# Three instead of four plain float32 units for each of the first two chunks, with a new order table

## The chip, the core and the metric

The kernel runs on one core of a Trainium2 chip. A core has five engines with queues of their own, each worked off strictly in order: TensorE (PE, matmuls into PSUM), VectorE (DVE), ScalarE (ACT), GpSimd (POOL) and SyncE (SP), which here only issues DMAs. The metric is the device time of one execution in microseconds; lower is better.

## What is computed

A local attention with block summaries, and a feed-forward layer on its result. Cut to what matters:

```python
B, H, S, D = 4, 8, 768, 64;  block, window = 32, 16;  scale = 1 / sqrt(D)
k_sum, v_sum = max of k, mean of v over each block of 32 positions
scores_l = scale * q @ k.T                 # only where |i - j| < window
scores_s = scale * q @ k_sum.T + log(block)
a = softmax(concat([masked scores_l, scores_s]))
x = (a @ concat([v, v_sum])).reshape(3072, 512)
h = x @ w_in                               # 512 -> 2048
out = (h * sigmoid(h)) @ w_out             # 2048 -> 512
```

The weights come in as float64 bit patterns. The kernel turns them into float32 on the chip, and then into scaled pairs of fp16 numbers (a high part and the rest).

## The kernel before

**Tiling.** The 3072 tokens are 24 stages of 128 (six for each batch element) and 12 chunks of 256. A stage is the attention of its 128 tokens, in four steps of two heads (`job_a`: scores, exponential, turning; `job_c`: the product with v; `job_x`: the result as an fp16 pair, xh and xl). The hidden width of 2048 is cut into eight pieces f = 0 to 7 of 256. A **unit** is one chunk with one piece (`job_f`, 96 units): two halves of the first product (line 908, 12 fp16 matmuls each), tanh on ScalarE (922), a multiply on VectorE (923), then the second product (917) in two calls, one for each 128 tokens, which adds to the chunk's output banks.

**Two kinds of units.** A unit can run its second product in two ways. The ordinary way casts the activations to fp16 (927), subtracts to get the rest (928), and multiplies fp16 pairs: three matmuls for each half. It needs the second weight as an fp16 pair, and all of these pairs share one scale `kap`, for which the sums of all eight second weights (line 836) and the largest values of all eight first weights (842/844, brought to all rows by the small matmul 848 and read by 852) must be there: lines 865 to 878, with a matmul of its own at line 868. The plain way needs no `kap`: it scales the float32 activations by the first weight's factor (925) and multiplies float32 by float32. The constant `QF` says for how many pieces the first two chunks use the plain way. These chunks run their pieces 0 to QF-1 first (chunk 0, then chunk 1), close the sum and put it aside (938), run the rest later (chunk 1, then chunk 0) and add the two sums (949). Chunks 2 to 11 run all pieces in one go, in fp16.

```python
    first = list(range(NFP))[:QF]
    rest = list(range(NFP))[QF:]
    runs = [(c, first) for c in range(NSUP)] + [(c, rest) for c in reversed(range(NSUP))]
    runs += [(c, first + rest) for c in range(NSUP, NCHUNK)]
    ...
        plain = c < NPW and f < QF
    ...
            terms = ((g, plain_w[f, 1]),) if plain else ((gh, wt[f, 1][:, 0]), (gh, wt[f, 1][:, 1]), (gl, wt[f, 1][:, 0]))
```

**Preparing a weight** (`job_w`): one DMA of 1 MB (816), three bit operations that make float32 of the two halves (826 on ScalarE, 822 on GpSimd, 820 on ScalarE or 824 on VectorE, 828 on VectorE), the sum or maximum, and the split into fp16 (`split_w`: 860 on ScalarE, 861 on VectorE; the profile shows them by the helpers' lines, 266 and 273). Unit f of the first product needs its first weight split; a plain unit needs its second weight as float32 only.

**The order.** The kernel first lists all its operations with their dependencies and with the engines that may run each (`plan.op`). The table `ORDER` then gives the sequence and the engine: three base-36 digits for each operation, five times its number plus the engine. `replay` walks the table, works out planned times from fixed costs, and puts filler matmuls (line 389) where TensorE would idle at the start. Each engine's queue has its operations in the order of the table. SP's queue holds all 276 DMAs. The dictionary `TUNE` feeds priorities that count only when no table of the right length is there.

**Shared places.** The small matmuls of the early part (848, 868, and those of the scales) write one PSUM bank, so each waits until the reader of the one before (852 for 848) is done. Weight pieces that are loaded late lend their memory to the first four stages for keys and values.

Of the kernel before, what the change touches and what calls it, by code (L numbers as in the profile page):

```python
# [251 lines left out]
def local_attn_ffn(ctx: ExitStack, tc: tile.TileContext, q0, qkT, qF, qD, kF, kD, v, vR, w, out):  # L252
# [782 lines left out]
    "12i0k30jt0k50iz0td12p0tj0km0jb0jj0kr0kw0uc0uf0l10kc0l40lu12v0fw0lc0g210l10q1nh0um11t1250ux10v0lz0md0no0ne0nu0mu0n00gp0kf"
    "0g81cw1nm0mk1nu0mq0n212y0nk0nw0v51md0v10n91mk0lg1201d10vi0o40vc1d91290vu0w11dd0o60on0w70od0p71dj1dv1e00oj1dl0ph0pd0pn0ot"
    "0pp0wa0wg0ur1e80vl0ov0q60wk0wn0qb0qg0pw0p30wu0x50xd0xq0x10y21n41dq0y91ec0lm0m91uz0pz0ql0qo1mt12f0yd0x91eu0qw0yi1101ei0ls"
    "1uw1ez0xk1f70yn14q14x0ys0yv0r00r61330z21ne1up1411ek1ep1fb1fh1nz1v71ud1690zd1530xt0z70vr16g0ra13a11311a1560zh14814e1vy1w4"
    "14h1fo0zl0zx1h216y1h71hf0zs1751hj1hp1o215b16m1ft1fy1fj1g61mn13b15g1um1ga17b1hw13i15j1j010118h18s18o1wa17e1gg1gn0xz16p107"
    "17k17q14n1wd1la1lm16v1wj1i11i61ie15q18x1931ii1io1hr1v91ve1vm16111l1m417r17y1971gi19c19f1vp19m19r19w1a11a61j51jd1vw1x71xd"  # L1040
    "1xj1o51om1oc1891oi1jh1mx1iv1jz1jn1q01n71pq1r215x1ab1q61ag1cp1ar1os16518d1ju11p1ws1wp1k41iq1wy1r911h2bs1ow2bn1p11p61pd1kc"
    "1kg2bi1ct1pg2bd1rj1zt1zy1pk1pw1qa13t13x1av1km1kt20x21213n1c51bv1bz1sx1x41lr1cf2061l61rp1jp1mb1ko20a20g20m1xm20s22122621a"
    "21e1y61yd1sn1st21k1qf1qp1xw1y31c92cc21o1qk1cj21w1qu1xt1yh1rf1rt1ym1ry1s31u51t31l122e1t718322i22o1qy1sa1bb2cr1yp1sd1sh1yw"
    "1tc1ti1tn1z11z61zb1h023523a23i1zg1zl1bl1zq2bz20n21r22s1bf23m23023s2cj22v1tr1tv1al2c323w2cn2dq2cy2441bp23z2d224b24l1tz2p3"
    "1b124w2501uf1lh2e12dw2p82pg2pk25325a25k2pq26o2pw25g2e524f26y2eg2q72eb2qc25q25u24p2d82qk2qo1gv25z26b2qu2r028028h28728d2db"
    "2dm2dh2ek2652q226e2rb2ng26u27427828n28r29l27d27k29v26i2rg2ro27o2gn2rs2px2r62sf2r127s2a129r2ry2sk2a52aa2al28w2eq2s427w2f3"
    "2ag2ap2at29729229b2ev29f2sa2fa2f02fd2ss2sw2t22fk2s52nn2c82fp2fu2hb2fz2g42ax2nv2hi2t82ho2b52hs2g92t91b52iu2b92hy2i22gs2gz"
    "2h42i72nr2jb2jh2j12j72ie2ij2im3ac2ha2iq3ah2kd3ap2ku2kk2te3bg2lw2l03at2tl2tv3bl3az3b53bb2of2ok2kq2l42l92o22o62lf2tp3bt3bx"
    "2jl2jq2tz2oc2k23ck2m33cp2md2u33c33c73cf3do2jv3cx2k530x3d12ua2uk3d72gg2uq2vm2os2ll3db2lo2ls2m92ug2uu2mj2mn3dt2ow2p031c3e1"
    "3e53143183b63eb2ms38p2vt2n43dj2w32my2n72nb3es2k92uz3ex3f52x52xc3f931w2xm2vz3213eh3ca3de2v92v52ve3en2vi3ff3fj2w92yo31j31n"  # L1050
# [120 lines left out]
```

## Time and profile before

| what | us |
|---|---|
| median of three runs | 612.56 (612.44 to 612.84) |
| the profiled execution | 612.63 |
| its span, first to last instruction | 610.9 |
| TensorE busy | 605.8 |
| VectorE busy | 466.9 |
| ScalarE busy | 391.5 |
| GpSimd busy | 139.7 |

The span is what the trace shows; 1.73 us of the execution's time lie around it. A busy time is the time in which at least one instruction of the engine ran, so the overlapping of pipelined matmuls is not counted twice, and the mean of a matmul's record is longer than the distance to the next. Pieces of the chain of waits show that distance. A line number is that of the kernel's text, for copies and scalings that of the helper (258 to 276).

### The profile page before, as it was taken

Reading aid. Unit: us, or ns where it says so; the run is one execution under the profiler, and the core shown is the slowest. Engines: PE = TensorE matmul, PEld = TensorE weight load, DVE = VectorE, ACT = ScalarE, POOL = GpSimd, SP = SyncE. Lnnn points to the kernel's source line nnn. Section 1 sums busy time; section 2 is a strip of 40 time slices with the busy share of each in tenths; the row PEclk is TensorE's granted clock in tenths of the full one; section 3 lists DMA queues with packets and bytes.
Section 4 is the critical chain, followed back from the end, with each engine's and each line's share of the span. In section 5 each row is a group of like instructions: output and inputs, shape, how many; then the busy total and the mean of one; then the engine's idle time right before and its main releaser. Section 6 shows DMA issues by size and latency. Waiting matters only on the chain.

```text
span 610.9 us, 13765 instructions
## 1 busy us (share of the span) xinstructions
PE 605.8 (99%) x5085; PEld 427.6 (70%) x5085; DVE 466.9 (76%) x1384; ACT 391.5 (64%) x866; POOL 139.7 (23%) x172
## 2 busy tenths in 40 slices
PE   8999999999999999999999999999999999999997
PEld 5786756677676776767777676767767667666785
DVE  7998978999889766897888846997788876753321
ACT  3999989667776667655787567644665655442222
POOL 2333321023314301413303341112422012101000
PEclk9999999999999999999999999999999999999999
DMA  8999615764666754583775764685565652502100
GB/s 310 342 335 382 248 40 167 172 158 114 191 137 141 202 172 142 158 210 82 195 145 130 173 194 136 152 197 124 98 161 130 143 131 64 87 14 57 53 2 35
DMA packets 91560, 93.50 MB, mean 153 GB/s; under 512 B 70348, under 2 KB 72652, under 8 KB 89444
## 3 DMA queue, kind: packets, MB, share of 16 engines
q1 hardware_dynamic: 91492, 92.62, 56.0%
q8 instruction: 40, 0.66, 0.5%
q14 instruction: 28, 0.23, 0.1%
HBM read 68.12 MB, written 6.29 MB: 122 GB/s over the span
## 4 chain that ended last, share of the span: by engine, by line
PE 94%; DMA 3%; ACT 1%; SPq 0%; DVE 0%; issue 0%
PE bank L917 42%; PE bank L908 41%; PE bank L762 4%; PE bank L676 2%; PE bank L677 2%; DMA wt<-in_w_dram 1%; DMA wt<-in_kF_dram 1%; PE bank L746 1%; DMA wt<-vms 1%; PE bank L674 1%; PE bank L671 0%; ACT wt L826 0%; ACT e L691 0%; PE bank L389 0%; PE bank L460 0%
## 5 line engine op out<-in xcount | busy, mean ns | idle before, releaser
L917 PE MATMUL bank<-wt,g 128*128 128x512 f16 (+2 forms) x1168 | 278.6, 382 | 0.0
L908 PE MATMUL bank<-xh,wt 128*128 128x256 f16 x1536 | 273.9, 273 | 0.0
L908 PEld LDWEIGHTS <-wt 128*128 128x128 f16 x2304 | 224.1, 98 | 45.1 <-issue 3.3
L908 PE MATMUL bank<-xl,wt 128*128 128x256 f16 x768 | 209.3, 273 | 0.0
L917 PEld LDWEIGHTS <-g 128*128 128x128 f16 x1104 | 106.7, 98 | 95.3 <-issue 0.8
L922 ACT ACTIVATE t<-bank,asc 128x512 f32<-128x512 f32 x96 | 65.7, 684 | 90.0 <-PE bank L908 89.7
L923 DVE SCALAR_TENSOR_TENSOR t<-t,bank 128x512 f32<-128x512 f32 x96 | 65.5, 683 | 55.7 <-ACT t L922 55.1
L691 ACT ACTIVATE e<-e,mx 128x182 f32<-128x182 f32 x192 | 83.8, 438 | 29.2 <-DVE mx L688 28.9
L927 ACT CAST g<-t 128x512 f16<-128x512 f32 x88 | 54.1, 615 | 49.4 <-DVE t L923 46.3
L726 DVE SCALAR_TENSOR_TENSOR p<-e,sum,p 128x128 f16<-128x128 f32 x320 | 80.1, 313 | 2.9 <-POOL p L715 1.7
L276 POOL TENSOR_TENSOR g<-t,g 128x512 f16<-128x512 f32 x31 | 35.9, 1158 | 161.3 <-ACT g L927 77.5
L688 DVE CUSTOM_DVE_ANT_0 e<-bank,masks,qsc 128x182 f32<-128x182 f32 x144 | 54.0, 402 | 21.0 <-PE bank L677 19.0
L715 POOL TENSOR_SCALAR p<-e,sum 128x182 f16<-128x182 f32 x45 | 24.6, 549 | 119.1 <-DVE sum L708 23.5
L276 DVE TENSOR_TENSOR g<-t,g 128x512 f16<-128x512 f32 x57 | 39.7, 696 | 12.0 <-ACT g L927 11.3
L691 ACT ACTIVATION_READ_ACCUMULATOR e<-e,mx 128x1 f32 x192 | 36.1, 188 | 0.0
L713 ACT ACTIVATE p<-e,sum 128x182 f16<-128x182 f32 x65 | 26.6, 437 | 14.1 <-DVE sum L708 7.4
L276 POOL TENSOR_TENSOR vv<-raw,vv 128x1024 f16<-128x1024 f32 x12 | 25.6, 2133 | 15.6 <-DVE p L717 5.9
L571 DVE SCALAR_TENSOR_TENSOR qk<-raw,qsc,qk 64x1264 f16<-64x1264 f32 x18 | 27.6, 1535 | 2.0 <-ACT qk L570 1.4
L676 PE MATMUL bank<-qk 128*128 128x182 f16 x144 | 28.7, 241 | 0.0
L677 PE MATMUL bank<-qk 128*128 128x182 f16 x144 | 28.7, 242 | 0.0
L570 ACT ACTIVATE qk<-raw,qsc 128x1264 f16<-128x1264 f32 x18 | 24.1, 1340 | 5.1 <-DMA raw<-in_kD_dram 5.1
L566 DVE SCALAR_TENSOR_TENSOR qk<-raw,qsc,qk 128x1024 f16<-128x1024 f32 x18 | 23.7, 1316 | 3.7 <-ACT qk L565 3.6
(169 smaller groups left out, 640.1 us busy)
## 6 DMA issues: line engine op xcount, KB each, us to landing
wt<-in_w_dram SPq DMA_DIRECT2D x16, 1024.0 KB
raw<-in_kD_dram SPq DMA_DIRECT2D x18, 632.0 KB
raw<-in_v_dram SPq DMA_DIRECT2D x20, 512.0 KB
raw<-in_qD_dram SPq DMA_DIRECT2D x18, 512.0 KB
out_dram<-raw SPq DMA_DIRECT2D x23, 256.0 KB
raw<-in_kF_dram SPq DMA_DIRECT2D x12, 384.0 KB
raw<-in_qF_dram SPq DMA_DIRECT2D x9, 512.0 KB
raw<-in_vR_dram SPq DMA_DIRECT2D x12, 384.0 KB
```

What stands on the lines that cost most here:

```text
L276: eng[e].tensor_tensor(out=out, in0=in0, in1=in1, op=ALU.subtract)
L571: plan.op({"dve": 1450}, lambda e: nc.vector.scalar_tensor_tensor(out=kst[64:, :, :NLOC], in0=kr[64:], scalar=qs[64:, 1:2], in1=kst[64:, : ...
L676: nc.tensor.matmul(out=sc[:, i, :NKEY], lhsT=qh[:, h, :], rhs=kst[:, h, :], start=True, stop=False)
L677: nc.tensor.matmul(out=sc[:, i, :NKEY], lhsT=ql[:, h, :], rhs=kst[:, h, :], start=False, stop=True)
L688: plan.op({"dve": 258 if b == 0 else 323}, lambda e, i=i: nc.vector.tensor_tensor_reduce(out=et[:, i, :NKEY], in0=sc[:, i, :NKEY], in1=mas ...
L691: plan.op({"act": 431}, lambda e, i=i, h=h: nc.scalar.activation(out=et[:, i, :NKEY], in_=et[:, i, :NKEY], func=AF.Exp, scale=-1.0, bias=m ...
L726: nc.vector.scalar_tensor_tensor(out=pt[:, i, to:to + z - a], in0=et[:, i, a:z], scalar=su[:, i:i + 1], in1=pt[:, i, a:z], op0=ALU.mult, o ...
L908: nc.tensor.matmul(out=h[:, d * CH:(d + 1) * CH], lhsT=wt[f, 0][:, part, d, ct * P:(ct + 1) * P], rhs=x[:, ct, :], start=(ct == 0 and q == ...
L917: nc.tensor.matmul(out=bank[to][:, :z0 - a0], lhsT=a[:, d * CH + u * P:d * CH + u * P + P], rhs=b[:, d, a0:z0], start=(opens and d == 0 an ...
L922: plan.op({"act": 640}, lambda e: nc.scalar.activation(out=t, in_=h, func=AF.Tanh, scale=asc_t[c // 3 % 2][:, f:f + 1]), r=[("bank", k), ( ...
L923: plan.op({"dve": 605}, lambda e: nc.vector.scalar_tensor_tensor(out=t, in0=t, scalar=1.0, in1=h, op0=ALU.add, op1=ALU.mult), r=[("bank", ...
L927: plan.op({"act": 540}, lambda e: nc.scalar.copy(out=gh, in_=t), r=[("t", j)], w=[("gh", n)], prio=at - TUNE["post"])
```

## The change

`QF` goes from 4 to 3. Piece 3 of chunks 0 and 1 is then an ordinary fp16 unit and is run with the late pieces: chunk 0 and chunk 1 each have three plain units and five ordinary ones. Each of the two units has two operations (927, 928) in the place of one (925), so the list has 2530 operations instead of 2528, and they are numbered anew. The early sums are closed behind piece 2 instead of piece 3.

`ORDER` is replaced as a whole. Read back by number, every operation runs on an engine that its `plan.op` allows, as before; the lists of allowed engines are not changed. Of the 2522 operations that both tables have, 204 go to another of their allowed engines. TensorE keeps 536 operations and SP 276; ScalarE goes from 642 to 653, VectorE from 926 to 912, GpSimd from 148 to 153. In SP's queue the 16 weights come in another sequence, and two key pieces of the second batch element stand among them earlier than before. The end of the table (chunk 11) differs in the order of the last calls, and two of its three last evictions move from ScalarE to VectorE.

```diff
-QF = 4
+QF = 3
...
 ORDER = (
-    "1lw00700l00r1lz00b00h01f01k00405p02401p02f01t05w02801507006q06206600v01b07601106c06e0av06w06m02j03d02u07807g07i02n07z085"
...
-    "9q09qn9qq9ow9qg9q59qx9r0"
+    "0041jc1jw00b1kd00h00l01f01k00r05p01p02001t06606q06c06w07005w06206e07601501b00v01102402f07802j02u00803d06m07i07z08t07g0av"
...
+    "9q59qm9qq9qa9qx9r09p69qf9r69ra"
 )
```

More of the change, by code (lines that the diff above doesn't have):

```diff
@@ L1035 @@
[L1035 to L1050, printed above, removed]
@@ new lines @@
+    "02807p07v0aq0b902n08j08p03s04302y0390850870bq08z0910bw03o0bg0bm0320by0ck09i09808f04d1k10d209n09s09x0re0rl05g03h03w0cq0ca"
+    "0cg0c50ed0ej0e30e90dj0dp0d90rr0df0ru0rz0el0cs0dr0dy0sx0b00ta0490et04g04n04s0t40s60f204x0f70520570fc0d005c0fh0gf0ga0gt0ha"
+    "0tm0tt0tz0hg0i40ia0s71uf0se0sl0hu0i00gk0h00h60a00sp0a705l09b0hi0ic0hq0ik0im0u20ac0ai0st11t10a0ao1200u70jx0it10h10n0j30jn"
+    "0k30fk0fr0ue0jt0j90td0b50lz0ev0k50iz0km0uf0kr0kw0jb0l11kn0kd0um0fw12i0l412612p0lu0jj0lb10q0md0mu0mk0no0g20ne12u0ux0g812y"
@@ new lines @@
+    "0gp1290kf0lg1lj1cw0nu0mq0n00n20m40v50vi0nk0nw0o30vc0na1d10o60v11dv1e010w1100ut1u00vu0p70w10ph1sf0w71d90od1lh0lm0pn1dd0pd"
+    "0m90on0pp0wa1lo0lq0ot0oj0q60ov0vl1dj1dl14q0wg1e81kz0wk0qb0p20pw1lw0qg0wn14x0wu0ql0y20y90x50qo1u60yf0x11ec1ei1kf0xd0tj0yi"
+    "0zl0yo0x90xo0xk0zs0zx1t90qv0pz0r00r61m10ys0xt1m41dq1eu14114814c1ez0ra1ep1531f70yv0z21fb0vr12f1ek1011l91fh16915616g16m1jo"
+    "11311a1g31g815b1gg18h1gk18o1fo1h218u1071331381s71h713b16p15g1fj13i18x15j1gq14h1gx1i116y17517a17e15q16v0z91tb1tg11h1to193"
@@ new lines @@
+    "1hf17j1i617q17r1gs1hj0zd0zh13p17y0xz14n19719c19f1hp1hw1kv1sn1ul1tt19m1kp1m719r1uc1xv1y019w1sz1l513t1a11a613x1ie1ur1v911l"
+    "1ab1ns1ag1ii1c51sh1ty1uu1me1io1mo1o21y81vf11p1vl1w81vo1yc1611an1mk1c91651mu1my1p41pl1yi1yo1v02at2ao1pb1iv1j81bl1bp1cf1cj"
+    "1yz1z42ay1v61wo1n31na1vy1zc1zg1o81ny1oc1hr1nd1bv1zm1iq1vv1oh1ot1on1yu2032081j21yp1bz1wf2bx1zq1zy1t11ow1w51ni1wj1wr1qz183"
+    "1k81qp1nm21720g1zt20k1wy15v21c1x31pr1x81xd1qv1ph1pv1q01r51r91xi1xn1re20q1xs1q61p02bi20u2122aj20x1qb1qf1rp1rk1rt18918d21k"
@@ new lines @@
+    "21o2bp2bt1qj22b22g21u21y2c42c81cp22o1rx1s12421b12cw1ct1fw24622122s2261jt1b524924g22y26423426a24q25u24w2602db2dm26e2o92oe"
+    "2b526j2d226v2om2oq2ow2p21sr23523h23l23a23r1ar24m27627d27n1av1g125025523v25h2d725b25k29128r2ch2ft2pd2pi2pq2pu2p827j27t27x"
+    "2822p32dh28x2cn2mm2qh2qm2q02q62qc2q726p1jj2972qu2cs2dq29b29g2rl2rq29r29m26y2qy2722b92ni2r429v1bb2dw2e92ra25o2rb2mt2e12eg"
+    "2e62ej28828d28h2rg2eq2ce2gh2sp2su2ry2s22ev2f02f529z2be2s82gy2h42go2gu2n12n82i02mx2fa2ff2h82sc2fy2hd2ih28l2a32i72jj2sk2sf"
@@ new lines @@
+    "2nc2k02jq2g52ga2ab2af2t23am2t62gg2nl2nq2ho2fk2hj2hs2l22l93ar2jw2lj2ud2tc2ti2in2k62id2to1bf2ir2iw2tj2lp2lf2j62j33bq3az3b3"
+    "3b92jb2uk2u52tv2nx2o22uu3bf3bv3c32ka3bl2kf2kk2kp2ku2o82vw2w32wd3cu3c73cd3cz3bg2xf2tz3ch3cp3ck2lt2jf3d72ly2m92u92m43db3dh"
+    "2md2xw2xm3173dn2w93dy2wj2wn31e2v031i2ws2uq2v42v92xs2y22y62yb3232hw2vk2vf2yy2vo31m3e33eb31t3dt2zf2zl2z52zb2wy2ky3ef3el3do"
+    "2x331x3f23f72zp38z32u2mh39v3ep3ex3g62x733b2zu3ff3013fj3fp33134d2yn33h3043gb3ft3g13es2yh2yq39e34k34u3963gj3gn30939l34q337"
@@ new lines @@
+    "39p35035433l35w36d3633gt3gz32632b3fw2vs33q3ha34036j37f33x34537m3593hf3hn3h53692xb35f2yu3hr30d30h36n34936s36y3h02fp37w39a"
+    "3k235k35o35s3qw3hx3i337432i32n32t39y30z37s30p3ie3kj3k93ll3a33ij31330t37737b3ls3m238238638b3ir3iv38n3i94473n438g38q3nb38u"
+    "3kf3j13j73nl3r33r73sk3kp44c3m83nh44k3i43on3j83kt3ky3la44o3l33ld44u4503ou3jd3ju3p43ly3lh45b45g3jy3jl4564513mc3jo3rv3nr3p0"
+    "3mh3ms3nv46f46k45o3aa45s45y3mm3mw3o03n03pa3pe3pj46246a3af3o63aj3rb3s03ob3of3oj46546s46w47247j47o3pq3sq3sw3pv3py3q247647e"
@@ new lines @@
+    "4793ri3rm47w3tt48048648c3s73tz3sz3u53us3t53q63tb48n48s3sd3sg3te48i4904943qo3qs49a49r49w3uz49e49m3tk4a44a83tq3v83u84ae3uf"
+    "4ak48d43h4av4b04aq4kw4b83rt4bz3ui4bc3up3v33vb3vi4bi4bo49h3wf4c43qe3qi3ww3x23vn3wm3xy3ws3yf42k4al3y542r4km42v4cc3yl3yb3x6"
+    "3xb3yp3xg42z4364bu3zh3zo4bp3vs4cg3zy43j43o43v43a4lg4kr4cm4cq3yu4y73xm3xq4104174yc4cy3zu4413z54yk4ct4kh41h4yo4yu4dg4dj3z1"
+    "3z94dn4e44d64d941d4yy4zb4ea4zg4mf4444lv3xu4du40440840d41n41r3vx3w23w741w4zo4zs40k3wc40o40s4z650f4f650k4zy5044fd4224e04fn"
@@ new lines @@
+    "4gp4274z142b4ee42f4gw50s50w50a51j4ln51o51251851e52n52s4mq4ml4no4h64i84m24h24lr51w4hc4m64ej4ep5054ev5205265194hg4nu4mu4ft"
+    "53040w4hl4hr4ey4nz4n94l352c52i53r52d4ip3zd4iv53w53453a53g4n04if53m4f24nf4o74fj4il4iz4j44jf4fx4g24gd4wz4hw4j94jj4jn4g84gh"
+    "4i04gl54v4n54x654454854e4l75505584i44xg4oe4pr4nk4pw4o44oh4jr4xa4oo4ot4oy4mc4qf54i4p354q4jz4lc4p84pd4q44qm4qw4ry4s54qs55z"
+    "4sf4r24r64rb4ri4wk4q84qe4xj4th4to4sl5644ty4v05fe4wr56c53h4k354l55c55i56g55m55u4u44rm4rq4v74tu4u856m4k94vd4kd4vh56q4sb4sp"
@@ new lines @@
+    "4ud4uo4su55p4ru4wv4vn4t14vr4t54t95nw5o15o94vw4w75eh5eo57n5od5oj4xo4uk4xw4y05844us4td56y4uw57u5805on57g57j5p05p55pd56t576"
+    "4pi5ph4y65pn59659d59n4w15ew4wb58a58e5ov5q44wf5pr58j5es5q959j59t59x58u5pz58p58y5qh5f35ap5b65aw5795a25r85m95c85b25ql5qr5rd"
+    "5oq5pu5rl5f75ac5cf5925cp5rp5qx5bc5bg5g45bl5r35qy5a85cl5ah5bv5cv5mo5cz5d45br5c05gb5gl5da5dg5dj5hn5mg5sc5i45hu5j65jd5jn5rv"
+    "5s15mv5gr5i05ia5ie5ij5sh5sp5st5gh5s25gv5fg5al5iu5io5h05h65hc5n55hf5kp5l65jj5s75jt5jx5k25sz5t35c45kc5k95dn5fl5kw5l25dr5e9"
@@ new lines @@
+    "5tg5tb5tl5mz6465mk5xc5iy5xt5xj5fs5fx5t65yv5g35tt5tx5n85nd5uk5up5u35u75uf5xp5lc5lg5ll5lr5ux5kh5kl64d5vo5z25zc5lv5zi60e5v1"
+    "5v75m060l5dz5e35vt5ed5w15w55ua5xz5wb5vd5vj60v61161x5y35y85hj5wf6hh5wn6hm5m46il64h5yj5nl5ye5yn5yr62462e5np6hu5nt64l60r5j2"
+    "6155ve65u61a62a61g6hy62k6iq5wi61m61p6i462o5x562t6i86ig6iy5x86j25wv5wy6336j861t63063863c6jc6536jp5z86ju5zm5zr5zw6jk6kt655"
+    "6ky6ib60260660a64s64w6k265a63g6696k66kc6606666736l665h6kg6la6lg65l65q66f66l6796ko6lx6lm66o6m26ma63o67i6me67f6826jf6mk6mq"
@@ new lines @@
+    "66u67067s67p6fu6y663s6ls6n16n66ne6ni6896gt67z6g96mw68i6o54pp6oa68d68l6gr6kj68s69p68x69263y6oi6om6a66ln6no6nu69w6b86a26ac"
+    "6ag6al6bp6bv6mr6nv6bf6bl6bz6cr6c46cy6ax6os6oy6d86o06aq6ce6gy6ea6g16de6b06eh6gg6gk6h56d46di6dn69769c6p96pe6cb6426er6b46pm"
+    "6pq6pw6g56y16q06dy6dt6e26oz6cj6ex6p47bh7bm6q87bu6ha6qx7by7c46he7ca6q36qg6qq6re7cl6rk6r46sg6sx6en6f16ra6f66fb6fg6sn6t37cq"
+    "6z56qj69h7cg69m7cy7d26tz6fl7d87de7dp7du6qt6u66ug7cb6vi7dk7df6xw6zc6zg6yq7e26yx7e66z17et7ey6st6t76cn6zp7ec6uc6zv6um6uq6xr"
@@ new lines @@
+    "6yd6ro6rt6uv6e67007ei6ry7eo6s47fx7ej6fp7f670j7g26tc70p6s86vz7fa7fg6w57fm7fs70470y70f7fn7196vp7147a96v16tj6sc6v66va6ve6vv"
+    "6w96we7h17ga7ge7gk7h66wp70a7317go6wk6wt6wx6tm6tr6tv70u7he6yh6zn7ar7hi71e71h71o7367gw6ym7i57ia7ag71r7ak71y7236x17ho7hs7i0"
+    "72872d6x972i72n6xj79u73p74673w6xn7ii7im7is73e73j7427j97je7jm6xd7rr7587gr75p75v73o7at74c75f76r76y77477877e75l7hv7ay7iy7jq"
+    "7j47a177i77n74g74l7jw7k078a81681b81j7k882a82f74v75z74q7507647iz7a575478h78n78r78x7kx76f81n76976j7k381t81x7le7kq8257b583e"
@@ new lines @@
+    "82n79182r7bb7be7s67l47mg83j82x8318397ry7s284i7967kg77y77t7827mx83r7zj79d7la7mn7sn79h83v84179l7nz7og76n7lk7n37o67lo7om845"
+    "7lt7kt7m57mt7n784n84v78684z82084d7m072s7nc7pi85m7m87pp7pz85r7nj8347oc7oq7ov7sd7sh7te8557nm85985h86q7p67p17pa7nr7tv7tl85z"
+    "7ux8637q57pv7q986v8487qe79p7qo7v47ve7wg86986f86l87u7va8738777vk87d7vo7qj7qt7wx7nv7wn7zy7xz87j7pe7zq7zu87z7x37vt8057wt7x7"
+    "7xc7tr7xm7u17u57ua7kj88785c87p88b7w57w088h7mc7w87ug8097qx7r17um7up88y8937sq86g88n88t7sv8ic80f7yg7y67yc7rj7rn8hg8am7ut7r9"
@@ new lines @@
+    "7t37t87rd89b89f7xi8b37wc8qv89l8at8c57td80i80n8b989p8r07xr8r88az8bd8bi89x8rz8bs7ym7yq7yv8cm7z687k8af8bo8cc8do8rc8ri7z27za"
+    "8e58eb8s48sc8rm88o8bx8c18cs8ci80v89s8108138hv8cw8a58hn8ru8t38rp8dv7ze8d17xv8t88f78a88sg8sm8sq8dc8sy8u78st8tg8tk8fe8uc8tq"
+    "8tu8u28e18ef8tx8vb8ai8fo8if8hr8ik8i28i68j38uk8uo8d78uu8dg8dk8fk72z8ek8uy8v68fu8v18fy8g38eu8g88ge8gi8jk8gm8ja8km8eq8ez8kt"
+    "8jg8jq8ju8vg8wf8wk8vo8vs8vy8ws8l38m58mm8f38w48gq8wa8ww8x28h88hc8ms8jz8pn8kb8pu8mc8l98mi8w58x68k48ke8no8xj8nv8p88pf8pj8q5"
@@ L1095 @@
+    "9f99er9em9fd9gk9fj9gp9gx9h19h79fp9fv9gc9gg9fq9hb9ht9hj9hy9ho9g39he9i69ia9ig9im9j29j79jf9is9ix9jj9jp9jt9kb9kg9ko9ks9ky9k1"
+    "9k69lk9in9lp9lx9l49la9jw9m19m79mb9lf9mt9mj9my9n69na9ng9nk9mo9g69o29o79of9l59oj9ns9nx9pb9op9ot9pg9po9ps9me9py9q29p19nn9ow"
+    "9q59qm9qq9qa9qx9r09p69qf9r69ra"
 )
```

50 lines of the change are left out of this document (4 added, 46 removed).

## The prediction, made before the changed kernel ran

> **What bounds the kernel now.** I read the page first: the span, the busy times and the shares of the chain that ended last.
>
> ```profile
> span 610.9 us, 13765 instructions
> ...
> PE 605.8 (99%) x5085; PEld 427.6 (70%) x5085; DVE 466.9 (76%) x1384; ACT 391.5 (64%) x866; POOL 139.7 (23%) x172
> ...
> PE 94%; DMA 3%; ACT 1%; SPq 0%; DVE 0%; issue 0%
> ```
>
> The reader is to see that TensorE sets the end: it is 94% of the chain. The rest is the first 33 us, which load and decode, and the last eviction and store. So a TensorE microsecond taken away after that start is a microsecond of the kernel, as long as nothing makes TensorE wait instead. Whether something will, is read from the stage in which the changed units lie: the windows of the early part (columns: length, then busy us and instructions of PE, PEld, DVE, ACT, POOL, granted clock, DMA share, GB/s).
>
> ```profile
> 0.00:20.00 20.00, 18.24 (x117) 10.80 (x117) 15.51 (x73) 10.80 (x36) 4.25 (x18) 1.00 0.92 327
> 20.00:40.00 20.00, 19.70 (x264) 16.69 (x264) 19.52 (x61) 19.70 (x48) 8.31 (x7) 1.00 0.92 330
> 40.00:60.00 20.00, 20.00 (x166) 14.48 (x165) 18.30 (x38) 18.82 (x34) 8.09 (x10) 1.00 0.96 365
> 60.00:80.00 20.00, 20.00 (x114) 13.16 (x115) 17.58 (x26) 19.65 (x32) 6.54 (x9) 1.00 0.59 221
> 80.00:100.00 20.00, 20.00 (x123) 13.14 (x122) 17.12 (x43) 17.92 (x32) 5.41 (x10) 1.00 0.36 100
> ```
>
> From 40 us on TensorE has no gap, at full clock. But in the same stretch the two engines that prepare its operands are nearly full too: from 20 to 80 us VectorE is busy 19.52 + 18.30 + 17.58 = 55.40 of 60 us, ScalarE 58.17. This is the one stage in which three engines run close together.
>
> **The term on TensorE.** The float32 units are pieces of line 917 before 103 us. The chain in order of time (start, length, what) has them, and an ordinary unit of 12 fp16 matmuls at 130 us.
>
> ```profile
> 59.88 0.12 PE bank L848 x2
> ...
> 72.17 1.72 PE bank L917 x4
> ...
> 78.34 1.82 PE bank L917 x4
> ...
> 94.12 1.72 PE bank L917 x4
> 95.84 2.62 PE bank L908 x24
> 98.46 4.73 PE bank L917 x14
> ...
> 130.28 2.59 PE bank L917 x12
> ```
>
> One call of the second product on a float32 unit is four records, 1.72 us, or 1.82 where a small float32 matmul stands in front. The calls that change are those of unit 3 in chunk 0 (72.17 and 78.34) and in chunk 1 (94.12, and the second of the three calls that make up the 14 records at 98.46: four, four and six, 1.72 + 1.72 + 1.29). They sum to 1.72 + 1.82 + 1.72 + 1.72 = 6.98 us. As fp16 units they are two times 2.59 = 5.18 us. **TensorE loses 1.80 us of work**, all of it on the chain. The first product (1.31 us for each half, from the 24 records in 2.62), the attention and the other 94 units keep their instructions.
>
> **The engines beside it.** Each of the two units has its float32 scaling on ScalarE (line 925) replaced by a cast there (927), a pass over the same tile, and a subtraction (928), which the new order gives to GpSimd both times.
>
> ```profile
> L276 POOL TENSOR_TENSOR g<-t,g 128x512 f16<-128x512 f32 x31 | 35.9, 1158 | 161.3 <-ACT g L927 77.5 <-PE bank L908 26.2 <-ACT xh L266 14.8
> ```
>
> That is 1.16 us more on the way from a unit's first product to its second. In chunk 1 the new order puts two halves of unit 4 (1.31 each) and two float32 calls (1.72 each) in between, 6.06 us, which covers it. I cost it at nothing; without the cover it is up to 1.16 us for each unit. The fp16 split of unit 3's second weight moves ahead of chunk 1: one pass each of ScalarE and VectorE, 1.28 us on VectorE (line 273 in the rows further down). It lands in 80 to 100 us, where VectorE idles 2.88 us and ScalarE 2.08; also nothing, at worst 1.28. The closing sums of the early half (line 938) come a unit sooner, in equal number.
>
> **The deadline that moves.** Every fp16 second weight waits for one scale over all weights (lines 865 to 878). Its matmul (868) stands in the middle of TensorE's queue, and whatever is behind it waits for the sums in front of it. The time line shows how it is met now.
>
> ```profile
> 78.85 0.16 DVE L866 TENSOR_REDUCE wom<-wo 128x1 f32<-128x8 f32 x1
> ...
> 80.00 0.38 PE L868 MATMUL bank<-ident,wom 128*128 128x128 f32 x2
> ```
>
> VectorE is done at 79.01, TensorE comes at 80.00: 0.99 us of slack. In the new order unit 3 of chunk 0 no longer stands ahead of 868 (2 x 1.31 + 1.72 + 1.82 = 6.16 us less), and one more half of unit 2 of chunk 1 does (1.31 more). TensorE would come at 80.00 - 6.16 + 1.31 = 75.15, that is 4.85 us sooner. VectorE's queue ahead of 866 shrinks only from 137 operations to 133. From 20 to 80 us its 125 instructions take 0.44 us each (55.40 / 125), so it is lighter by up to 1.8 us; since longer ones come as others leave, I take 1.0. If it kept every one of its pauses, the matmul would be 4.85 - 1.0 - 0.99 = 2.9 us later than TensorE wants it. If the pauses close (4.60 us of them from 20 to 80), it costs nothing. Bounds: 0 and 2.9. Behind a TensorE that is 4.85 us earlier the pauses that wait for its results shrink, and with DMA at 0.92 in the first 40 us there is some 3 us of earlier arrival to be had, so I take a value near the lower end, 0.5 us. ScalarE's queue ahead of the last of lines 836 shrinks from 100 operations to 91 and is the looser one.
>
> **Sum.** 612.63 us of the profiled execution (span 610.9 and 1.73 around it) - 1.80 + 0.5 = 611.3. That execution lay 0.07 over the median of 612.56, so **611.2**.
>
> **Rivals.** *The deadline takes the gain back* (no change): the pauses close only by half, TensorE waits 1.3 us at 868, and 612.56 - 1.8 + 1.3 = 612.1. For it: 0.99 us of slack against 4.85. Against it: the pauses that follow TensorE's pace.
>
> *VectorE gets stuck behind a transfer* (slower). In the new order VectorE's operation 110 is line 824 on unit 5's second weight, and the next but one is 852 of unit 3, which frees the bank that TensorE's 848 of unit 4 writes (59.88 in the chain above, with the same work ahead of it in both orders). All of chunk 1 stands behind that 848. The transfer is the 45th in SP's queue.
>
> ```profile
> wt<-in_w_dram SPq DMA_DIRECT2D x16, 1024.0 KB
> ```
>
> Thirteen such transfers are 13.6 MB, and with what the attention has loaded by then I estimate 20 MB; the windows moved 20 us x (327 + 330 + 365) GB/s = 20.4 MB by 60 us. So it lands at about 59, and three operations at 0.44 later TensorE may go, at 60.3 against 59.9: 0.4 us. If it lands after 60, VectorE's queue up to 866 bites. It still holds six of line 828, three maxima, three of line 923 and one split.
>
> ```profile
> L923 DVE SCALAR_TENSOR_TENSOR t<-t,bank 128x512 f32<-128x512 f32 x96 | 65.5, 683 | 55.7 <-ACT t L922 55.1
> ...
> L828 DVE SCALAR_TENSOR_TENSOR wt<-wt 128x1024 uint32<-128x1024 uint32 x16 | 19.8, 1244 | 0.4 <-POOL wt L822 0.4
> ...
> L273 DVE SCALAR_TENSOR_TENSOR wt<-wt,uk 128x1024 f16<-128x1024 f32 x8 | 10.2, 1277 | 0.0
> ...
> L842 DVE TENSOR_REDUCE wm<-wt 128x1 f32<-128x1024 f32 x6 | 7.3, 1214 | 0.0
> ```
>
> 6 x 1.244 + 3 x 1.214 + 3 x 0.683 + 1.277 = 14.4 us: from 61.3 it ends at 75.7, with 2 to 3 us of pauses 868 comes near 78.4, 3.3 us late: 612.56 - 1.8 + 3.3 = 614.1. It decides from a landing at 60 us on. Against it: 59 us is the old queue's pace, with its idle stretches in it (DMA share 0.92).
>
> *TensorE slows down after such a wait.* The time line has fillers (line 389) from the start and from a pause.
>
> ```profile
> 1.43 4.60 PE L389 MATMUL bank<-ident 128*128 128x256 bf16 x21 [1.43 <-POOL ident masks.py:199]
> ...
> 34.48 1.27 PE L389 MATMUL bank<-ident 128*128 128x256 bf16 x10
> ```
>
> At the start one takes 219 ns (4.60 / 21), at 34 us 127 ns (1.27 / 10). If the wait is so long that the next 4.6 us of work go at the first pace, they cost 4.6 x (219 / 127 - 1) = 3.3 us more: 617.4. The Trainium skill (TensorE: Matmul & The Clock Gate, section "What's actually happening") says that the array's clock halves after an idle window of about 3.4 us and comes back after as long a busy one. The first row agrees with that; no row here shows a relapse.
>
> *The start gets shorter too* (faster): fillers mark waits, and the ten at 34.48 stand for 1.2 us in which TensorE waits for other engines. Without it: 611.2 - 1.2 = 610.0.
>
> **Chances.** Forecast 0.36 (its own range 610.6 to 611.3), shorter start 0.10, gain taken back 0.33, stuck behind the transfer 0.18, with the slow clock 0.03. About 0.2%, 1.2 us, is what a measurement of this kernel can tell from no change. Faster 0.46, within 0.2% 0.33, slower 0.21. The range runs from a little under the shorter start, 609.6, to a little over the transfer's price, 614.2, and takes in both ends of the deadline (610.8 and 613.7).
>
> **What would show it.** Right: 48 float32 and 1032 fp16 records of 512 columns at line 917; TensorE at 868 between 75 and 76 us; no TensorE idle over 0.5 us after 40 us; the stretch behind chunk 1 as long as before. Wrong: an idle piece in front of 848 of unit 4 or of 868; VectorE idle at line 824 with a weight transfer as releaser; a granted clock under 1.00 between 60 and 90 us; or new waits after 130 us, which I have costed at nothing because VectorE, the fullest engine beside TensorE, is 76% busy over the span.

## The result and the profile after

The changed kernel is slower by 1%. Its median is 619.67 us of 4 runs (617.65 to 621.22), against 612.5 of the kernel before beside it (612.13 to 612.84). The ratio is 1.0105, with a 95% interval of 1.0082 to 1.0129. The forecast of 611.2 us was wrong, and so was the range up to 614.2. The new runs also scatter over 3.6 us, the old ones over 0.7.

The profiled execution took 619.25 us. The page of the changed kernel has the busy times and the chain that ended last:

```profile
span 617.5 us, 13766 instructions
...
PE 606.9 (98%) x5103; PEld 427.4 (69%) x5103; DVE 461.2 (75%) x1370; ACT 400.6 (65%) x878; POOL 137.7 (22%) x177
...
PE 80%; DMA 11%; DVE 4%; ACT 3%; issue 1%; SPq 1%; POOL 0%; ACTq 0%; POOLq 0%; DVEq 0%
```

TensorE's share of the chain fell from 94% to 80%, and DMA's rose from 3% to 11%. So the end is no longer set by TensorE's work alone: somewhere it waits for transfers. Where it does is seen in the windows (length, then busy us and instructions of PE, PEld, DVE, ACT, POOL, granted clock, DMA share, GB/s). Before:

```profile
200.00:300.00 100.00, 100.00 (x852) 70.76 (x850) 77.21 (x234) 65.28 (x149) 24.67 (x24) 1.00 0.61 165
300.00:400.00 100.00, 100.00 (x853) 70.63 (x851) 77.72 (x244) 69.80 (x159) 25.67 (x25) 1.00 0.64 162
400.00:500.00 100.00, 100.00 (x848) 70.15 (x847) 82.78 (x258) 56.54 (x133) 21.48 (x27) 1.00 0.61 138
```

After:

```profile
200.00:300.00 100.00, 98.12 (x832) 68.84 (x831) 76.43 (x223) 67.31 (x150) 21.02 (x24) 1.00 0.63 166
300.00:400.00 100.00, 97.90 (x828) 67.96 (x827) 73.72 (x230) 68.93 (x152) 17.51 (x21) 1.00 0.64 154
400.00:500.00 100.00, 99.42 (x844) 69.92 (x843) 79.20 (x249) 58.18 (x138) 24.55 (x27) 1.00 0.55 136
```

TensorE has gaps 100 to 400 us behind the place of the change, at full clock, while no other engine is full. The chain of the changed kernel in order of time (start, length, what) shows the largest one, 369.59 us:

```profile
358.42 3.21 DMA raw<-in_kF_dram
...
362.68 0.94 ACT raw L443 x2
...
363.64 4.47 DMA raw<-in_qF_dram
...
369.16 0.20 ACT raw L451
...
369.38 0.17 DVE qm L452
...
369.59 0.71 PE bank L460 x4
```

These are `job_k` and `job_scale` of batch 3. Four key and three query tiles go one after another through the three `raw` buffers; ScalarE sums absolute values (443, 451), VectorE adds the sums (452, 453), and a small matmul (460) spreads the result over the partitions. That matmul stands in TensorE's queue, and everything behind it waits. A load starts when ScalarE lets a buffer go: the key tile lands at 361.63, ScalarE is through with it at 363.62, and at 363.64 the next load counts. VectorE's line 452 shows who waits for whom, first in the kernel before, then after (three instructions, one for each batch; duration in ns, then first and last start):

```profile
L452 DVE TENSOR_REDUCE qm<-qm x3: 143/155/155, 105.2 to 371.3; 128x1 f32<-128x3 f32 x3
its engine sat idle before it (us, times) until:
  ACT raw L451: 0.7, 1
```

```profile
L452 DVE TENSOR_REDUCE qm<-qm x3: 155/155/156, 96.7 to 369.4; 128x1 f32<-128x3 f32 x3
its engine sat idle before it (us, times) until:
  ACT raw L451: 4.1, 3
who waited for it (us, times):
  PEld bank L460: 3.1, 2
  PE bank L460: 2.5, 2
```

Before, nobody waits for it. After, TensorE does for 2.5 us of idle time (2.9 by the measure that follows, which goes by starts: the end of the record ahead of a gap lies outside the idle time).

To add such waits up, I call TensorE's **delay** at a call its start less the durations of all calls ahead of it in its queue (1.31 us for half of a first product, 1.30 and 1.72 for an fp16 and a float32 call, the others from their rows). It grows only where TensorE waits, and by 0.13 to 0.15 a chunk through rounding.

| delay, us | first call of chunk 0 | of chunk 2 | of chunk 5 | at the end |
|---|---|---|---|---|
| before | 11.7 | 13.3 | 13.7 | 14.6 |
| after | 12.3 | 15.5 | 17.5 | 22.9 |

That gives the sum of the profiled executions. Up to chunk 2 the changed kernel waits 15.5 - 13.3 = 2.2 us more, from there on (22.9 - 15.5) - (14.6 - 13.3) = 6.1 us more, and it has 1.8 us less work: +6.5, and the spans differ by 6.6. The late part is in single steps: 0.5 and 0.3 at 221 to 223 us (the first behind ScalarE's cast, line 927), 0.7 at line 460 of batch 2 (230 us), 1.05 at the start of chunk 5 (295), 0.3 at 365 and 2.2 at line 460 of batch 3 (370), 0.8 in chunk 7 (420, behind a transposing DMA). The one at 295 us is another transfer, stage v's, with GpSimd and ScalarE behind it:

```profile
287.03 4.68 DMA raw<-vms
...
291.89 1.13 POOL raw L628
...
293.05 1.05 ACT vv L258
...
294.54 0.58 ACT raw L266
...
295.16 1.46 PE bank L917 x6
```

### The profile page after: what moved, and what is told of

Its sections match the earlier page's. It is cut to its first block, busy times and chain, and to the rows that moved or that the text cites. A ratio compares the mean times of both kernels' runs of the same rounds, so it can differ in the third digit from the quotient of the medians.

```text
span 617.5 us, 13766 instructions
## 1 busy us (share of the span) xinstructions
PE 606.9 (98%) x5103; PEld 427.4 (69%) x5103; DVE 461.2 (75%) x1370; ACT 400.6 (65%) x878; POOL 137.7 (22%) x177
## 4 chain that ended last, share of the span: by engine, by line
PE 80%; DMA 11%; DVE 4%; ACT 3%; issue 1%; SPq 1%; POOL 0%; ACTq 0%; POOLq 0%; DVEq 0%
PE bank L917 35%; PE bank L908 33%; PE bank L762 3%; DMA wt<-in_w_dram 3%; DMA raw<-in_kF_dram 2%; PE bank L676 2%; PE bank L677 2%; DMA raw<-in_qF_dram 1%; PE bank L671 1%; DMA raw<-vms 1%; PE bank L389 1%; PE bank L600 1%; DMA raw<-in_kD_dram 1%; DMA raw<-in_v_dram 1%; DMA tt<-p 1%
## 5 line engine op out<-in xcount | busy, mean ns | idle before, releaser
L917 PEld LDWEIGHTS <-g 128*128 128x128 f16 x1128 | 108.9, 98 | 101.5 <-issue 1.4
L276 POOL TENSOR_TENSOR g<-t,g 128x512 f16<-128x512 f32 x41 | 47.5, 1159 | 199.4 <-ACT g L927 102.7
L715 POOL TENSOR_SCALAR p<-e,sum 128x182 f16<-128x182 f32 x42 | 18.6, 445 | 112.1 <-DVE sum L708 37.2
L276 DVE TENSOR_TENSOR g<-t,g 128x512 f16<-128x512 f32 x49 | 34.0, 693 | 11.6 <-ACT g L927 11.2
L713 ACT ACTIVATE p<-e,sum 128x182 f16<-128x182 f32 x76 | 31.3, 439 | 13.7 <-ACT e L691 4.6
L762 PEld LDWEIGHTS <-vv 128*64 128x64 f16 x800 | 22.7, 110 | 4.0 <-issue 3.4
L762 PE MATMUL bank<-tt,vv 128*64 128x128 f16 x800 | 24.6, 220 | 0.6 <-DMA tt<-p 0.6
```

The source lines that it names most:

```text
L276: eng[e].tensor_tensor(out=out, in0=in0, in1=in1, op=ALU.subtract)
L762: nc.tensor.matmul(out=to[j * D:(j + 1) * D, i * P:(i + 1) * P], lhsT=vs[w][:, vi, h * D:(h + 1) * D], rhs=tt[:, j * 3 + blk, :], start=(n ...
L917: nc.tensor.matmul(out=bank[to][:, :z0 - a0], lhsT=a[:, d * CH + u * P:d * CH + u * P + P], rhs=b[:, d, a0:z0], start=(opens and d == 0 an ...
```

## Experiments

Theory A: the new order's part behind chunk 2 sets the transfers and the sums of batches 2 and 3 too close to the TensorE calls that need them, and the three float32 units have nothing to do with it. Theory B: the early part is the cause, the missing float32 unit and its deadline, and the late waits follow from what it leaves behind. Both kernels plan the same operations under nearly the same names, so an order table can be put together from the two. Below, P is a half of a first product (line 908), W a call of the second (917), with chunk and unit.

All results, with medians, ratios to the kernel before beside them, and the growth of the delay in the profiled execution:

| kernel | us | ratio (95%) | to chunk 0 | to chunk 2 | to chunk 5 | to the end |
|---|---|---|---|---|---|---|
| before | 612.5 to 613.3 | | 11.7 | 1.6 | 0.4 | 0.9 |
| after | 619.7 | 1.0105 (1.0082 to 1.0129) | 12.3 | 3.2 | 2.0 | 5.4 |
| early_new_late_old | 617.8 | 1.0081 (1.0067 to 1.0094) | 13.1 | 5.6 | 0.4 | 0.9 |
| early_old_late_new | 622.9 | 1.0180 (1.0156 to 1.0205) | 10.9 | 4.1 | 7.0 | 2.6 |
| switch_at_chunk5 | 614.7 | 1.0032 (1.0019 to 1.0044) | 13.4 | 2.4 | 2.0 | 1.0 |
| scale_two_later | 621.5 | 1.0141 (1.0127 to 1.0154) | 13.7 | 2.9 | 4.5 | 4.4 |
| late_old_from_chunk3 | 615.1 | 1.0035 (1.0023 to 1.0047) | 13.6 | 3.1 | 1.1 | 0.9 |
| late_new_from_chunk3 | 618.0 | 1.0089 (1.0071 to 1.0106) | 11.1 | 1.7 | 3.8 | 3.1 |
| half_query_transfers | 616.9 | 1.0062 (1.0049 to 1.0075) | 13.8 | 3.1 | 1.0 | 2.5 |
| start_old_middle_new | 619.0 | 1.0104 (1.0088 to 1.0119) | 11.0 | 6.0 | 3.1 | 2.5 |
| start_old_stage3_moved | 616.6 | 1.0065 (1.0049 to 1.0081) | 11.3 | 8.3 | 2.2 | 0.9 |
| stage3_moved | 616.5 | 1.0070 (1.0047 to 1.0093) | 12.7 | 4.9 | 1.0 | 1.1 |
| three_units_chunk1_only | 615.1 | 1.0043 (1.0025 to 1.0061) | 11.5 | 4.6 | 0.4 | 0.9 |
| chunk1_evict_later | 613.3 | 1.0005 (0.9988 to 1.0022) | 11.4 | 2.5 | 0.6 | 0.9 |
| chunk1_subtract_on_dve | 612.5 | 0.9987 (0.9971 to 1.0003) | 13.2 | 1.9 | 0.4 | 2.0 |

### Which part of the order

```diff
 early_new_late_old (QF = 3)
-the new table
+the new table's operations up to the first P of chunk 2, then all others as the old table has them
 early_old_late_new (QF = 4)
-the old table
+the old table's up to the first P of chunk 2, then all others as the new table has them
 switch_at_chunk5 (QF = 3)
-the new table
+the new table's up to the first P of chunk 5, then all others as the old table has them
```

> This is the kernel after (three float32 units) in its own order up to the first product of chunk 2, and the order of the kernel before from there on. Theory A (the late part of the new order sets the transfers and sums of batches 2 and 3 too close to the TensorE instructions that need them; the change of the early chunks is about even): 612.5 - 1.8 of float32 calls + 2.2 of waits before chunk 2 = 612.9 us, 612 to 614, and no TensorE wait over 0.5 us after 150 us. Theory B (the early part is what costs, and the late waits follow from the state that it leaves behind): 617 to 620 us with the late waits still there.

617.8 us. By the number alone that is theory B's range. But theory B has the late waits still there, and they are not: TensorE waits twice at the switch itself (2.2 us at 145 us and 0.8 at 147), and never after it. These are the windows of that run:

```profile
200.00:300.00 100.00, 100.00 (x851) 70.59 (x849) 77.90 (x236) 65.89 (x151) 23.52 (x25) 1.00 0.60 157
300.00:400.00 100.00, 100.00 (x850) 70.31 (x848) 77.31 (x241) 70.41 (x157) 28.12 (x26) 1.00 0.63 164
```

With the new early part and the old late part TensorE is full again, and the delay grows by 0.4 and 0.9 as in the kernel before. So the late waits don't follow from the early part.

> The mirror of the run before: four float32 units and the order of the kernel before up to the first product of chunk 2, the order of the kernel after from there on. Theory A: 612.5 + 6 to 7 us of late waits (0.5, 0.3 and 0.7 in chunk 3, 1.0 at the start of chunk 5, 2.4 at the scale of batch 3, 0.8 in chunk 7) = 618.5 us, 616.5 to 620. Theory B: 612 to 613.5 us.

622.9 us, above theory A's range and far from theory B's. The switch costs some 7 us here (waits at 145 to 154 us). Behind it, waits of the new order are there with four float32 units too: 0.6 and 0.3 at 227 to 229 us, 0.5 and 1.6 at line 460 of batches 2 and 3. The one at the start of chunk 5 isn't.

> The kernel after in its own order up to the first product of chunk 5, and the order of the kernel before from there on. Theory A in the form that each wait is local to its place in the order: the waits of chunk 3 stay (1.5 us), those at the start of chunk 5, at the scale of batch 3 and in chunk 7 go (4.3 us): 615.2 us, 614 to 616.5. Theory B: 618 to 620 us. If the waits of the second half depend on those of the first, 613 to 614 us or 619 us.

614.7 us, in the range of theory A: the waits of chunk 3 stay (2.0 us up to chunk 5), those of chunks 5 to 7 are gone. So the late waits go with the late part of the order. How long each one is depends on what runs ahead of it, too: the one at the start of chunk 5 is 1.05 us in the changed kernel, 0.3 in two runs further down, and missing with the old early part. Theory B falls with these three as the account of the late waits; of the early part's own price more below.

A switch that costs less was found where the two tables have done almost the same operations, at the fifth unit of chunk 3.

```diff
 late_old_from_chunk3 (QF = 3)
-the new table
+the new table's up to the fifth unit of chunk 3, then all others as the old table has them
 late_new_from_chunk3 (QF = 4)
-the old table
+the old table's up to the fifth unit of chunk 3, then all others as the new table has them
```

> As early_new_late_old, but switched where the two orders stand almost at the same operations (the fifth unit of chunk 3: ten operations of the new order are ahead there, one of the old), so that the switch itself costs little. Theory A (late part of the order): 612.5 - 1.8 of float32 calls + 2.2 to 3 of waits ahead of chunk 2 = 612.9 to 613.7 us, 612 to 614.5, and no TensorE wait over 0.5 us behind the switch. Theory C (any switch of orders costs some microseconds, and the smooth second half of the runs before was luck of the place): 616 us or more.

615.1 us: the late waits are gone but for 0.7 us at the switch (222 to 224 us), which counts against theory C. Over the kernel before beside it that is 2.0 us, against 7.2 for the changed kernel. It is over theory A's range (up to 614.5) and under theory C's (from 616): the early part cost more here than theory A took (table: 13.6 + 3.1 against 11.7 + 1.6), and the kernel before was itself 613.05 us beside this run.

> The mirror: four float32 units and the order of the kernel before up to the fifth unit of chunk 3, the order of the kernel after from there on. Theory A: 612.5 + 4 to 6 us of late waits (chunk 3, scale of batch 2, start of chunk 5, scale of batch 3, chunk 7) = 617.5 us, 616 to 619. Theory B (the late waits come from what the early part leaves behind): 612 to 613.5 us.

618.0 us, as theory A has it. But about half of it is at the switch, where TensorE waits for a transposing DMA, so this run alone would prove little:

```profile
215.72 0.75 PE L762 MATMUL bank<-tt,vv 128*64 128x128 f16 x20 [3.00 <-DMA tt<-p]
```

The 1.4 us at line 460 of batch 3 and 0.7 in chunk 7 are the new order's.

### Is it the transfer or TensorE's queue?

```diff
 scale_two_later: TensorE's queue around the scale of batch 3; batch 2 alike
-P c6 f6, 460, W c6 f2, scores, W c6 f3, scores, W c6 f4, W c6 f5, scores, W c6 f5, scores
+P c6 f6, W c6 f2, W c6 f3, 460, W c6 f4, scores, W c6 f5, scores, W c6 f5, scores, P c6 f7, scores
```

> The kernel after with the scale matmul of batch 2 and of batch 3 (line 460) two calls later in TensorE's queue, and the four score calls behind each of them later by the same step; nothing else is moved. Theory A, local: the two waits at line 460 (0.7 and 2.2 us in the profile) are covered by 2.6 us of other products each: 616.5 us, 615.5 to 617.5. Rival: the loads of the keys and queries are late by themselves, and what is behind the scale waits in its stead: 619 us or more. Theory B says nothing else than 619 us.

621.5 us, worse than the changed kernel, as the rival had it. Nobody waits at line 460 any more, but the scores and casts behind it do, as in TensorE's time line of this run (idle us and who ended it in brackets):

```profile
240.59 0.24 PE L676 MATMUL bank<-qk 128*128 128x182 f16 x1 [0.94 <-DVE mx L688]
242.81 0.60 PE L917 MATMUL bank<-wt,g 128*128 128x512 f16 x2 [0.44 <-ACT g L927]
244.41 1.04 PE L917 MATMUL bank<-wt,g 128*128 128x512 f16 x4 [1.00 <-DVE g L276]
```

VectorE and ScalarE are in-order queues too. They hold the sums at the old place, stand there for the same transfer, and now the later scores come in a bunch. Moving the call that waited did not help here, where the thing waited for was late.

```diff
 half_query_transfers
-qf = stg[:, :2 * DM]
+qf = stg[:, :DM]
 ...
-nc.sync.dma_start(out=qf, in_=qF[b - 1, :, j, :])
+nc.sync.dma_start(out=qf, in_=qF[b - 1, :, j, :DM])
```

> The kernel after, in its own order; the three query transfers of line 450 of each batch bring half the columns, and line 451 sums half (half of the queries are left out of the scale's sum). If the chain of transfer and sum is what TensorE waits for at line 460 (0.7 and 2.2 us) and the order only sets where that chain ends: each of these transfers and sums becomes 1.5 to 2.5 us shorter, both waits go, 619.5 - 2.5 to 3.5 = 616.5 us, 615.5 to 617.5. If TensorE's own order, or VectorE's, sets these waits (as the run with the scale matmul two calls later allows): 618.5 to 621 us.

This kernel leaves half of the queries out of the scale's sum. 616.9 us, as expected of the transfers. Line 452 in this run, in the same view as above:

```profile
L452 DVE TENSOR_REDUCE qm<-qm x3: 150/156/156, 98.0 to 366.9; 128x1 f32<-128x3 f32 x3
its engine sat idle before it (us, times) until:
  ACT raw L451: 1.7, 1
```

Nobody waits for it now; 4.1 us of VectorE's idle time have become 1.7. Order and operations are those of the changed kernel, so the chain of load, sum and next load is what TensorE waits for at line 460, and the order decides when that chain ends. Load and sum became shorter together, so their shares aren't told apart. The step of chunk 3 shrinks as well, from 0.8 to 0.3 us. That at the start of chunk 5 is 0.35 us here, and 0.3 in scale_two_later, whose transfers are whole. The 0.75 us of chunk 7 stay; the halved tiles aren't in those, and of that wait only this is shown: it goes with the new order.

### The early part

With the new order the delay at the first call of chunk 0 is 12.3 to 13.8 us in seven of these kernels, with the old one 10.9 to 11.7 in seven of eight (13.2 in the eighth). From there to chunk 2 it grows by 2.4 to 3.2 where the new early part is whole and the switch lies behind it, against 1.6 and 1.7. The largest step is at 47 to 53 us, the attention of stage 3. Three runs tried to mend these.

```diff
 start_old_middle_new (QF = 3)
-the new table up to the fifth unit of chunk 3
+the old table's up to the first P of chunk 1, then the new table's up to the fifth unit of chunk 3
 start_old_stage3_moved (QF = 3)
+the old table's up to the first P of chunk 0, then as stage3_moved
 stage3_moved: TensorE's queue in chunk 0; old table from the fifth unit of chunk 3 on
-transposes of line 700 (m14), W c0 f0, 848 of unit 2, 791 of stage 3, 746, W c0 f0
+W c0 f0, transposes (m14), 848 of unit 2, W c0 f0, 746, 791 of stage 3
```

> Three float32 units; the order of the kernel before up to the first product of chunk 1 and again from the fifth unit of chunk 3 on, the new order between. If the early loss is the new order's start (0.6 to 1.9 us ahead of the first product of chunk 0, and 1.2 us at the attention of stage 3 near 50 us) and not the missing float32 unit: 612.5 - 1.8 + 0.7 of waits between chunks 1 and 2 = 611.4 us, 610.5 to 612.3, faster than both kernels. If the float32 unit itself is what covered something (the deadline of line 868 among it): 613 us or more.

> Three float32 units; the order of the kernel before up to the first product of chunk 0 and again from the fifth unit of chunk 3 on, the new order between, in which the calls of lines 746 and 791 of stage 3 are put behind the second call of unit 0 (line 917) and one transpose behind its first, as in the kernel before. Local reading of the waits at 47 to 51 us (0.4 + 0.2 + 0.6): 612.5 - 1.8 + 0.7 to 1.0 = 611.5 us, 610.7 to 612.5. If VectorE's queue is late there by itself, the waits move to the next call: 612.5 us or more.

> As late_old_from_chunk3 (615.07 us), with one place of the early part put as in the kernel before: the calls of lines 746 and 791 of stage 3 behind the second call of unit 0 in chunk 0, one transpose behind its first. Local reading of the waits near 50 us (0.4 + 0.2 + 0.6): 614.0 us, 613.4 to 614.6. If VectorE's queue is late there by itself: 614.8 to 616 us.

619.0, 616.6 and 616.5 us: all three are slower than the local reading had it. The old start is shorter by about 1.5 us where it was used, but what comes behind it then waits. The likely reason, not shown, is that the old start loads and decodes the weights for another sequence of calls. In start_old_stage3_moved TensorE waits for ScalarE near 48 us (0.9 us for the exponential, line 691, and 0.8 for a scaled activation, line 266). In start_old_middle_new the longest wait is at the 848 of unit 6, in TensorE's time line:

```profile
71.16 0.38 PE L848 MATMUL bank<-wm,spread 128*128 128x2 f32 x2 [1.94 <-DVE ur L852]
```

In stage3_moved the wait at line 791 is gone, and two waits for VectorE come behind it:

```profile
56.30 0.39 PE L908 MATMUL bank<-xh,wt 128*128 128x256 f16 x2 [0.70 <-DVE wt L273]
...
63.16 0.38 PE L848 MATMUL bank<-wm,spread 128*128 128x2 f32 x2 [0.62 <-DVE ur L852]
```

Both are VectorE's work on weights. Two more, 0.4 us at 48 us and 0.5 at 67, are for activations that ScalarE scales (line 266). So moving the one call does not mend it; which of the two queues sets this stretch is not shown. Why the new start is longer than the old one stays open.

### One float32 unit less without the new order

The float32 unit 3 of chunk 1 alone can go in the old order, since line 868 stands ahead of it there.

```diff
 three_units_chunk1_only (order and table of the kernel before)
-plain = c < NPW and f < QF
+qf = (4, 3)[c] if c < NSUP else QF
+plain = c < NPW and f < qf
 ...
-opens, closes = f == 0 or (split and f == QF), f == NFP - 1 or (split and f == QF - 1)
+opens, closes = f == 0 or (split and f == qf), f == NFP - 1 or (split and f == qf - 1)
 chunk1_evict_later, ScalarE's and TensorE's queues
-938 (u0), 927 c1 f4, 922 c1 f5, 927 c1 f5;   P c1 f6, W c1 f3 (u0), W c1 f5 (u1)
+927 c1 f4, 922 c1 f5, 927 c1 f5, 938 (u0);   P c1 f6, W c1 f5 (u1), W c1 f3 (u0)
 chunk1_subtract_on_dve
-928 c1 f4 on GpSimd
+928 c1 f4 on VectorE
```

> The kernel before in its own order, with three float32 units in chunk 1 alone (chunk 0 keeps four): unit 3 of chunk 1 gets the split form, its call for the second half of the rows goes four calls later, and the split of the second weight of unit 3 takes the place of that of unit 0, which comes later. One part of the change without the new order. If the float32 unit is worth what the calls last (2 x (1.72 to 1.82) - 2 x 1.30) and nothing else moves: 612.5 - 0.9 = 611.7 us, 611.2 to 612.3, a ratio of 0.9978 to 0.9992. If the earlier need of line 868 or of the split takes it back: 612.5 to 614 us.

615.1 us, slower than both readings had it, with two waits of TensorE inside the call of unit 4 (line numbers are one higher in these kernels):

```profile
101.58 0.61 PE L918 MATMUL bank<-wt,g 128*128 128x512 f16 x2 [1.29 <-ACT g L928]
102.82 1.04 PE L918 MATMUL bank<-wt,g 128*128 128x512 f16 x4 [0.64 <-POOL g L276]
```

The first was a copy on ScalarE (938), placed ahead of the cast that unit 4 waits for; the next run moves it.

> As three_units_chunk1_only, in which ScalarE stood 1.5 us at the copy of the first rows' partial sums (line 938, which waits for the last float32 call) ahead of the cast that unit 4 waits for, and TensorE with it 1.45 and 0.8 us. Here that copy stands behind the cast of unit 5, and unit 3's call for these rows three calls later; nothing else is moved. If that placement was the whole of the loss: those two waits go (2.3 us) and 0.9 us of float32 calls are saved against the kernel before, 612.0 to 612.8 us, a ratio of 0.9975 to 0.9995 to it. If the missing float32 unit costs by itself: no better than 614 us, with a wait in another place near 100 us.

613.3 us against 613.0, no change to be told. The first wait is gone, the second is left:

```profile
100.60 1.04 PE L918 MATMUL bank<-wt,g 128*128 128x512 f16 x4 [0.59 <-POOL g L276]
```

In the kernel before, three calls of line 917, two of them float32, run over this stretch, from 98.46 to 103.19 (the chain in the prediction has them), and GpSimd's subtraction for unit 4 ends under them, at 100.24 in the time line of the kernel before:

```profile
99.08 1.16 POOL L276 TENSOR_TENSOR g<-t,g 128x512 f16<-128x512 f32 x1
```

The shorter and later call takes that cover away: the delay steps by 0.8 us here, of the 0.9 saved.

> As chunk1_evict_later, with one subtraction (unit 4 of chunk 1) on VectorE instead of GpSimd, right behind the cast it waits for; in the run before, VectorE stood idle for 1.27 us at that place, and TensorE waited 0.59 us for GpSimd's subtraction of 1.16 us. If that subtraction is what took the 0.9 us of float32 calls back: TensorE waits 0 to 0.1 us there, 613.3 - 0.6 to 0.8 = 612.6 us, 612.1 to 613.0, and a ratio to the kernel before of 0.998 to 0.9998. If the float32 unit's time cannot be had because all of that stretch is as long as VectorE's and ScalarE's queues: 613.1 to 613.8 us, the wait now at the next call.

612.5 us against 613.1, as expected of the subtraction: the step in the delay falls from 0.8 to 0.2 us, and VectorE does the subtraction in 0.69 us in a gap of its own:

```profile
101.08 0.69 DVE L276 TENSOR_TENSOR g<-t,g 128x512 f16<-128x512 f32 x1 [0.69 <-ACT g L928]
```

With 0.9987 (0.9971 to 1.0003) its ratio is the lowest here, though the interval doesn't exclude no change. The missing float32 unit of chunk 0 was not run by itself. (Its profiled execution was one of its longer ones, 614.77 us, with 0.8 us at line 460 of batch 3: the old order, too, has little slack at that call.)

## Why the prediction was wrong

**TensorE's term, -1.80 us: right.** The two forms of line 917 in the groups by form (busy us, mean ns), before and then after:

```profile
L917 PE MATMUL bank<-wt,g 128*128 128x512 f16 x1008 | 237.5, 379 | 0.0
...
L917 PE MATMUL bank<-wt,g 128*128 128x512 f32 x64 | 30.3, 602 | 0.0
```

```profile
L917 PE MATMUL bank<-wt,g 128*128 128x512 f16 x1032 | 242.5, 379 | 1.5 <-ACT raw L266 0.9 <-ACT g L927 0.4
...
L917 PE MATMUL bank<-wt,g 128*128 128x512 f32 x48 | 23.0, 606 | 0.0
```

48 and 1032 records, as predicted. The sum above closes with 1.8. TensorE's busy time rose all the same, from 605.8 to 606.9 us: there are ten more fillers (57 records of line 389 for 9.4 us, against 47 for 8.3), and the end of a matmul's record, which the next matmul covers as a rule, counts by itself ahead of a gap.

**The edits costed at nothing: right in this order.** No step of the delay over 0.3 us lies between 53 and 200 us. That the cover counts was shown elsewhere: in the old order one subtraction of 1.16 us on GpSimd took back 0.8 of 0.9 us.

**The deadline at 868, +0.5 us: too much.** The time line after:

```profile
76.05 0.16 DVE L866 TENSOR_REDUCE wom<-wo 128x1 f32<-128x8 f32 x1
...
77.07 0.38 PE L868 MATMUL bank<-ident,wom 128*128 128x128 f32 x2
```

VectorE is done at 76.21, 0.86 us ahead of TensorE; the step of the delay is 0.1. TensorE came at 77.1 and not between 75 and 76, because it had lost time before 53 us.

**The rivals.** The deadline did not take the gain back. VectorE did not hold 848 of unit 4, since TensorE has no wait at line 848 in the changed kernel; the mechanism is real, though (1.94 us at 848 of unit 6 in start_old_middle_new). The granted clock is 1.00 where the slow clock would have shown, and TensorE is busy throughout there. In the changed kernel:

```profile
60.00:80.00 20.00, 20.00 (x115) 12.80 (x114) 18.50 (x34) 20.00 (x33) 8.54 (x14) 1.00 0.45 164
80.00:100.00 20.00, 20.00 (x128) 13.36 (x129) 19.20 (x59) 19.18 (x42) 6.19 (x6) 1.00 0.54 157
```

The shorter start went the other way: the delay at the first call of chunk 0 is 0.6 us longer in the profile, and up to 2.1 in the other runs of that order.

**The step that failed** is the last one: that the stretch behind chunk 1 would be as long as before, new waits after 130 us costed at nothing because VectorE, the fullest engine beside TensorE, is 76% busy over the span. They are 6.1 us, and VectorE's share is still 75%. A mean share of busy time says nothing of a chain that passes from a transfer to ScalarE to the next transfer; no engine in it is full. And the order behind chunk 1, which I took to be as good as the old one, was new as well. In the old one the same sum ends 0.27 us before TensorE gets to it, at 371.42 in the time line of the kernel before:

```profile
371.27 0.15 DVE L452 TENSOR_REDUCE qm<-qm 128x1 f32<-128x3 f32 x1
...
371.69 0.61 PE L460 MATMUL bank<-ident,qm 128*128 128x128 f32 x4
```

After, the sum ends even earlier, at 369.55 us, but TensorE was due there at 367.4 (369.59 less its wait of 2.2), 4.3 us earlier than before. That slack was to be had from the trace, and so were the new places of these operations from the diff: line 460 stands four (batch 2) and six (batch 3) TensorE calls earlier, counted from the first call of chunk 2. The second, smaller miss is the start and the attention up to 53 us, which the prediction took to be as long as before: 2.2 us, of which only the places are shown, not the cause.

## What to carry to other kernels

When a written-out order is replaced as a whole, every cross-engine wait in it is a part of the change. List the calls of the bounding engine that wait for another engine, with the slack that each has in the old trace, and see which ones the new order moves forward, however far from the edit they stand. Work taken off the bounding engine is gained only if what ended under that work has slack; moving the call that waited did not help here, because the thing it waits for came no sooner.
